# First rounds of attention in another order: second keys and queries loaded ahead of v, unit 2's scores ahead of v's pooling, weights converted later

## The chip, the core and the metric

The kernel runs on one NeuronCore of a Trainium2 chip. Five engines each work through their own list in order: TensorE (PE in the profile, PEld for its weight loads), VectorE (DVE), ScalarE (ACT), GpSimd (POOL), and SyncE (SP), whose queue issues the DMAs. Semaphores tie them together. The metric is device time in microseconds (us) of one execution; before the change the median of three runs is 660.65 us (657.95 to 663.04).

## What is computed

```python
def _attn_ref(q, k, v):                     # (2, 8, 576, 64)
    q_d, k_d, v_d = (t.reshape(B, H, Sd, 4, D).mean(axis=3) for t in (q, k, v))
    out_up = np.repeat(sm_attn(q_d, k_d, v_d), 4, axis=2)
    mask = np.abs(pos[:, None] - pos[None, :]) < 4
    scores = np.where(mask, scale * q @ k.T, -1e9)
    return out_up + softmax(scores) @ v
def reference(...):
    x = attn_out                            # 1152 tokens x 512
    h = x @ w_in                            # 512 -> 2048
    x = (h * clip(h + 3, 0, 6) / 6) @ w_out
    return sum(p[:, e] * (relu(x @ w1[e]) @ w2[e]) for e in range(4))
```

Two batches of eight heads. Each head has a local attention (each token sees the three before and after it) and a pooled one over means of four tokens; the sum goes through one wide MLP and then four weighted ones.

## The kernel before, in words

Products that need fp32 accuracy are made of a high and a low half of each operand (`three`: high-high, high-low, low-high). The long part of the run is the MLPs, one unbroken row of such matmuls. The change lies ahead of it, in the attention.

**Units and rounds.** A unit is two heads of one batch: eight units, 0 to 3 of batch 0, 4 to 7 of batch 1. Keys and queries are loaded for two units at a time (a pair, `load_k`, `load_q`; pair 0 in two pieces), v for a batch in three tiles (`load_v`, six to nine DMAs). A unit's work is cut into steps, and the loop over `t` (rounds 0 to 9) writes the steps of up to four units beside each other:

- `sums`: pooled keys and queries (sums of four), on POOL, or for the keys of the first units on DVE.
- `masks`, `scores` (L594, L607): local scores in PSUM, over a mask. `pooled_scores` (L670).
- `pooled_softmax` (L683 to L695), `less_max` (L624 to L631), `normalise`, `pooled_normalise`: maxima and sums on DVE, exponentials on ACT, the multiplications by the reciprocal on POOL.
- `turn` (L654), `pooled_turn` (L724): transposes on PE, copied to SBUF by ACT (`aT`, `aTd`).
- `values` (L744, L755): both attentions times v; then ACT copies the pooled part (`pd`), DVE adds (`xf`, L769), ACT rounds to the high half of x, and `low` (L785) makes the low half on DVE.
- `pool_v` (L463): sums of four rows of v, 18 matmuls for a batch, copied by ACT (L471). Its PSUM room is the single buffer called "last", which `values` and the idle products of round 1 use too; all else rotates through three buffers.

In these phases the order on PE, DVE, ACT and POOL is the order in which the program is written. SP's order is made by a scheduler. `idle_products(ps, n)` puts n matmuls of zeros (L551) into PE's list; nothing reads them.

**Conversion.** Each 1 MB tile of `w_in` arrives in a packed form and goes through a generator (`converting`) of four steps a tile: L237 on DVE with L213 on ACT; L247 on DVE; L259 and L268 on DVE with the high half on ACT (L221); the low half on DVE (L226). `convert(n)` runs the next n steps. Weight 0 is first needed by the matmuls of `pieces(1)` in round 8, weight 1 in round 9. The two first tiles are loaded in halves (`load_half`); these and the loads of the second batch are held: a one-element write of DVE (`hold`, L181) at the place where `load_next` calls them has to come before the DMA.

## Time and profile before

| | |
|---|---|
| median of three runs | 660.65 us |
| the profiled execution | 657.16 us, of which the trace spans 655.0 us |
| PE busy | 647.4 us (99%) |
| DVE, ACT, POOL busy | 415.9, 253.3, 95.3 us |
| granted TensorE clock, mean | 1.000 |

A busy PE here includes idle products, which do nothing for the result. The attention's rounds fill about the first 76 us.

### The profile page before, as it was taken

The page shows a single profiled execution, that of the slowest core. Times are in us where ns is not written, and L with a number is a line of the kernel's source. Part 1 is how long each engine was busy: PE and PEld are TensorE (multiplying, and loading weights), DVE is VectorE, ACT ScalarE, POOL GpSimd, SP SyncE. Part 2 cuts the span into 40 slices and gives each one's busy share as a digit, 9 for nine tenths or more (in the row PEclk, how much of TensorE's full clock was granted, in tenths as well). Part 3 has the DMA queues.
Part 4 walks back from the last instruction along what each step waited for, and adds up shares of the span by engine and source line. Part 5 has one row for each costly group of instructions (what it writes and reads, how often), then busy time and mean ns, then how long its engine had stood idle before and what let it go on. Part 6 is the DMA issues. An engine that isn't in the chain of part 4 may idle for free.

```text
span 655.0 us, 11972 instructions
## 1 busy us (share of the span) xinstructions
PE 647.4 (99%) x4929; PEld 582.6 (89%) x4943; DVE 415.9 (63%) x839; ACT 253.3 (39%) x591; POOL 95.3 (15%) x142
## 2 busy tenths in 40 slices
PE   8999999999999999999999999999999999999997
PEld 4657999999999999998998998998998988988985
DVE  6578899852794247585665665665765665755742
ACT  5567577442554246343233232241341331331410
POOL 4762000000000062101201201201201201201000
PEclk9999999999999999999999999999999999999999
DMA  8772333300510110300110110110210300200012
GB/s 278 226 236 91 130 124 134 129 1 1 193 66 1 65 64 1 131 2 0 65 65 1 65 65 1 65 65 1 87 43 0 129 2 15 115 1 2 2 48 97
DMA packets 12147, 45.89 MB, mean 70 GB/s; under 512 B 1334, under 2 KB 3382, under 8 KB 8252
## 3 DMA queue, kind: packets, MB, share of 16 engines
q1 hardware_dynamic: 12092, 45.12, 20.3%
q8 instruction: 39, 0.64, 0.4%
q14 instruction: 16, 0.13, 0.1%
HBM read 42.76 MB, written 2.36 MB: 69 GB/s over the span
## 4 chain that ended last, share of the span: by engine, by line
PE 96%; DMA 2%; SPq 1%; issue 0%; POOL 0%; DVE 0%; POOLq 0%
PE bank L936 27%; PE bank L1205 10%; PE bank L1206 10%; PE bank L1204 10%; PE bank L374 10%; PE bank L376 10%; PE bank L375 10%; PE pair L744 2%; PE pair L551 1%; DMA slot<-in_qT_dram 1%; PE pair L755 1%; DMA slot<-in_v_dram 1%; PE pair L607 1%; PE pair L724 1%; PE pair L670 1%; PE pair L654 1%
## 5 line engine op out<-in xcount | busy, mean ns | idle before, releaser
L936 PEld LDWEIGHTS bank<-xop,slot 128*128 128x128 f32 x1344 | 180.9, 188 | 1.3
L936 PE MATMUL bank<-xop,slot 128*128 128x288 f32 x1344 | 181.8, 295 | 0.0
L1205 PE MATMUL bank<-slot,h 128*128 128x512 f32 x288 | 113.9, 395 | 0.0
L1206 PE MATMUL bank<-slot,h 128*128 128x512 f32 x288 | 113.9, 395 | 0.0
L1204 PE MATMUL bank<-slot,h 128*128 128x512 f32 x288 | 113.8, 395 | 0.0
L1212 DVE SCALAR_TENSOR_TENSOR slot<-bank,pr,slot 128x512 f32<-128x512 f32 x63 | 47.3, 751 | 85.8 <-PE bank L1206 85.8
L442 POOL TENSOR_TENSOR st<-slot 128x256 f32<-128x256 f32 x16 | 13.9, 868 | 467.4 <-DMA slot<-in_w_dram 220.5
L1206 PEld LDWEIGHTS bank<-slot,h 128*128 128x128 f32 x288 | 54.1, 188 | 13.0
L1205 PEld LDWEIGHTS bank<-slot,h 128*128 128x128 f32 x288 | 54.1, 188 | 12.4
L1204 PEld LDWEIGHTS bank<-slot,h 128*128 128x128 f32 x288 | 54.1, 188 | 12.3
L376 PE MATMUL bank<-h,slot 128*128 128x384 f32 x192 | 64.7, 337 | 0.0
L375 PE MATMUL bank<-h,slot 128*128 128x384 f32 x192 | 64.7, 337 | 0.0
L374 PE MATMUL bank<-h,slot 128*128 128x384 f32 x192 | 64.7, 337 | 0.0
L374 PE MATMUL bank<-x,slot 128*128 128x384 f32 x188 | 63.1, 336 | 0.0
L376 PE MATMUL bank<-x,slot 128*128 128x384 f32 x188 | 62.9, 335 | 0.0
L375 PE MATMUL bank<-x,slot 128*128 128x384 f32 x188 | 62.9, 335 | 0.0
L442 DVE TENSOR_TENSOR u<-bank,u 128x288 f32<-128x288 f32 x96 | 43.6, 454 | 20.4 <-PE bank L936 20.0
L965 ACT ACTIVATE h<-c 128x288 fp32r<-128x288 f32 x64 | 27.9, 445 | 71.6 <-DVE c L442 71.5
L304 ACT ACTIVATE slot<-st 128x512 fp32r<-128x512 f32 x32 | 19.2, 624 | 64.6 <-POOL st L298 64.6
L825 DVE TENSOR_TENSOR h<-slot,h 128x384 fp32r<-128x384 f32 x48 | 27.5, 585 | 24.2 <-ACT h L824 24.1
L816 ACT ACTIVATE t<-bank,half__145 128x384 f32<-128x384 f32 x47 | 27.1, 581 | 40.1 <-PE bank L376 40.1
L817 DVE SCALAR_TENSOR_TENSOR slot<-t,bank 128x384 f32<-128x384 f32 x47 | 25.8, 552 | 24.5 <-ACT t L816 24.3
(115 smaller groups left out, 920.1 us busy)
## 6 DMA issues: line engine op xcount, KB each, us to landing
slot<-in_w_dram SPq DMA_DIRECT2D x16, 1024.0 KB, 4.8
slot<-in_w_out_dram SPq DMA_DIRECT2D x8, 1024.0 KB, 4.8
slot<-in_w_in_dram SPq DMA_DIRECT2D x6, 1024.0 KB, 5.3
slot<-in_v_dram SPq DMA_DIRECT2D x6, 512.0 KB, 4.8
out_dram<-slot SPq DMA_DIRECT2D x9, 256.0 KB, 2.0
slot<-in_w_in_dram SPq DMA_DIRECT2D x4, 512.0 KB, 5.9
slot<-in_kT_dram SPq DMA_DIRECT2D x3, 576.0 KB, 5.6
slot<-in_qT_dram SPq DMA_DIRECT2D x6, 288.0 KB, 6.0
```

The costliest lines, as they stand in the source:

```text
L374: nc.tensor.matmul(ps, wh, xh, start=first, stop=False)
L375: nc.tensor.matmul(ps, wh, xl, start=False, stop=False)
L376: nc.tensor.matmul(ps, wl, xh, start=False, stop=last)
L442: eng.tensor_tensor(out=out, in0=a, in1=b, op=ALU.add)
L816: nc.scalar.activation(out=t, in_=ps, func=AF.Relu, bias=half_, scale=1.0 / (6.0 * UP))
L825: nc.vector.tensor_tensor(out=g[:, 1, :], in0=u, in1=r32(g[:, 0, :]), op=ALU.subtract)
L936: nc.tensor.matmul(ps, a[:, i, k], b[:, j, k], start=start and k == 0 and n == 0, stop=stop and k == 1 and n == 2, skip_group_check=True,)
L965: nc.scalar.activation(out=self.h[:, 0, i, j], in_=of, func=AF.Relu)
L1204: nc.tensor.matmul(ps, hh, w[:, 0], start=(f == 0), stop=False)
L1205: nc.tensor.matmul(ps, hh, w[:, 1], start=False, stop=False)
L1206: nc.tensor.matmul(ps, hl, w[:, 0], start=False, stop=(f == NF - 1))
L1212: nc.vector.scalar_tensor_tensor(out=to, in0=ps, scalar=share, in1=to, op0=ALU.mult, op1=ALU.add)
```

## The change

In the first four rounds the steps stand in another order; in all rounds the loop is written out anew. `BY_DVE` is 4, and `sums` is split into `sums_k` (keys; on DVE for units 0 to 3) and `sums_q` (queries, on POOL).

```diff
     load_qk(0, 0, 1)
     load_qk(0, 1, 1)
+    load_qk(1)
     for p in range(NP):
         load_v(0, p)
-    load_qk(1)
...
-                if self.u < 2:
+                if self.u < BY_DVE:
                     nc.vector.tensor_reduce(out=to, in_=k4[:, r, : NI - r], op=ALU.add, axis=AX.X)
...
     later = [
-        lambda: load_half(0, 0),
-        lambda: load_half(0, 1),
         lambda: load_v(1, 0, (0,)),
         lambda: load_v(1, 0, (1,)),
         lambda: load_v(1, 1, (0,)),
-        last_v,
         lambda: load_k(NU // 2 - 1, held=True),
         lambda: load_q(NU // 2 - 1, held=True),
+        last_v,
+        lambda: load_half(0, 0),
+        lambda: load_half(0, 1),
         lambda: load_half(1, 0),
         lambda: load_half(1, 1),
     ]
...
+        elif t == 1:
+            n.pooled_scores(4)
+            n.masks(0)
+            n.scores()
+            n.pooled_softmax()
+            units[0].pooled_normalise()
+            load_qk(2)
+            units[2].sums_q()
+            n.less_max()
+            n.normalise()
+            n.pooled_normalise()
+            units[2].sums_k()
+            units[3].sums_k()
+            units[3].sums_q()
+            units[0].turn(0)
+            idle_products(banks(True), 8)
+            units[0].pooled_turn()
+            n.turn(4)
+        elif t == 2:
+            n.masks(0)
+            n.scores()
+            n.pooled_scores(0)
+            n.less_max()
+            n.pooled_softmax()
+            load_next()
+            n.normalise()
+            n.pooled_normalise()
+            load_next()
+            units[1].pooled_turn()
+        elif t == 3:
+            n.pooled_scores(0)
+            pool_v(0)
+            n.masks(0)
+            n.scores()
+            n.pooled_softmax()
+            units[4].sums()
+            n.less_max()
+            load_next()
+            n.normalise()
+            units[0].values()
+            units[2].turn(0)
+            units[2].pooled_turn()
+            n.pooled_normalise()
+            load_next()
+            units[5].sums()
+        elif t < NU:
+            n.pooled_scores(4)
+            n.masks(0)
+            n.scores()
+            n.pooled_softmax()
+            load_next()
+            n.less_max()
+            if t == NHP + 1:
+                pool_v(1)
+                convert(2)
+            units[0 if t == NHP else t - 3].low()
+            n.pooled_normalise()
+            n.normalise()
+            load_next()
+            if t < NU - 2:
+                units[t + 2].sums()
+            if t == NHP:
+                units[1].values()
+            units[t - 1].turn(4)
+            units[t - 2].values()
+            if t == NHP:
+                units[1].low()
+            units[t - 1].pooled_turn()
+            convert(1 if t > NHP else 0)
+            load_next()
...
```

Before, every round from 1 to 7 had the second form without its special cases, `pool_v(0, 8)` stood in round 1, `values` of unit t-2 in round t from 2 on, and `convert` ran 2 steps in round 3, one each in rounds 4 to 7, and 3 each in rounds 8 and 9; now it runs 3, 1, 1, 4 and 3 in rounds 5 to 9. Both make 12 steps. The idle products in PE's list were 71 and are 59: round 1 has 16 (before: 4, and 8 ahead of the pooling), rounds 2 and 3 have none (before: 8 each), rounds 4 to 7 have 8 each as before. At the end of round 4, PE has in both forms done the same work otherwise.

SP's queue, from the second load of pair 0's keys on; `in_kT_dram 128x2x576` is a pair's keys, `in_qT_dram 128x2x288` half a pair's queries. Before:

```order
L391 DMA slot<-in_kT_dram 128x576
L401 DMA slot<-in_qT_dram 128x288 x2
L410 DMA slot<-in_v_dram 48x512
L410 DMA slot<-in_v_dram 64x512
L410 DMA slot<-in_v_dram 128x512
L410 DMA slot<-in_v_dram 128x2x512 x3
L410 DMA slot<-in_v_dram 48x512
L410 DMA slot<-in_v_dram 32x512
L410 DMA slot<-in_v_dram 3x512
L391 DMA slot<-in_kT_dram 128x2x576
L401 DMA slot<-in_qT_dram 128x2x288 x4
```

Now:

```order
L393 DMA slot<-in_kT_dram 128x576
L403 DMA slot<-in_qT_dram 128x288 x2
L393 DMA slot<-in_kT_dram 128x2x576
L403 DMA slot<-in_qT_dram 128x2x288 x2
L412 DMA slot<-in_v_dram 48x512
L412 DMA slot<-in_v_dram 64x512
L412 DMA slot<-in_v_dram 128x512
L412 DMA slot<-in_v_dram 128x2x512 x3
L412 DMA slot<-in_v_dram 48x512
L412 DMA slot<-in_v_dram 32x512
L412 DMA slot<-in_v_dram 3x512
```

Pair 1's three loads (1152 KB) stand ahead of the nine loads of v's first batch (2182 KB) instead of behind them.

DVE's list in round 4, from unit 4's pooled denominators on; `den` to `rec` are of unit 4's softmax, `xf` is the sum that frees the PSUM room of `values`. Before:

```order
L706 TENSOR_SCALAR den_792<-smd_776 72x4
L710 RECIPROCAL recd_794<-den_792 72x4
L636 TENSOR_REDUCE sm_797<-ex1_125 128x10
L638 RECIPROCAL rec_799<-sm_797 128x10
L181 MEMSET slot_782 1x1
L769 TENSOR_TENSOR xf_871<-pair_828,pd_869 128x5x64
L769 TENSOR_TENSOR xf_871<-pair_828,pd_869 128x4x64
L247 SCALAR_TENSOR_TENSOR slot_712<-slot_445,slot_712 128x512 x2
```

Now:

```order
L718 TENSOR_SCALAR den_718<-smd_705 72x4
L722 RECIPROCAL recd_720<-den_718 72x4
L648 TENSOR_REDUCE sm_723<-ex1_125 128x10
L650 RECIPROCAL rec_725<-sm_723 128x10
L183 MEMSET slot_555 1x1
L438 MEMSET slot_730 6x512
L781 TENSOR_TENSOR xf_783<-pair_740,pd_781 128x5x64
L781 TENSOR_TENSOR xf_783<-pair_740,pd_781 128x4x64
L781 TENSOR_TENSOR xf_848<-pair_805,pd_846 128x5x64
L781 TENSOR_TENSOR xf_848<-pair_805,pd_846 128x4x64
```

There are two `xf` (of units 1 and 2) instead of one, and a hold and the zeroing of v's last rows (L436, now L438) stand between the reciprocal and the first of them.

DVE's list in rounds 7 and 8; L237 to L226 (now L239 to L228) are conversion. Before, weight 0's L226 stands a round earlier and is not in the piece, and `slot_1489` is weight 1:

```order
L769 TENSOR_TENSOR xf_1367<-pair_1324,pd_1365 128x5x64
L769 TENSOR_TENSOR xf_1367<-pair_1324,pd_1365 128x4x64
L237 TENSOR_SCALAR slot_1230<-slot_889 128x1024
L785 TENSOR_TENSOR x_78<-xf_1367,x_78 128x576
L817 SCALAR_TENSOR_TENSOR slot_1404<-t_1402,pair_1389 128x384
L769 TENSOR_TENSOR xf_1449<-pair_1406,pd_1447 128x5x64
L769 TENSOR_TENSOR xf_1449<-pair_1406,pd_1447 128x4x64
L247 SCALAR_TENSOR_TENSOR slot_1230<-slot_889,slot_1230 128x512 x2
L259 TENSOR_SCALAR slot_1230<-slot_1230 128x1024
L268 TENSOR_TENSOR slot_1230<-slot_1230 128x512 x2
L237 TENSOR_SCALAR slot_1580<-slot_1481 128x1024
L226 TENSOR_TENSOR slot_1489<-slot_1230,slot_1489 128x512 x2
```

Now, with `slot_1210` weight 0 and `slot_1476` weight 1:

```order
L781 TENSOR_TENSOR xf_1347<-pair_1304,pd_1345 128x4x64
L228 TENSOR_TENSOR slot_1210<-slot_953,slot_1210 128x512 x2
L797 TENSOR_TENSOR x_78<-xf_1347,x_78 128x576
L829 SCALAR_TENSOR_TENSOR slot_1390<-t_1388,pair_1375 128x384
L781 TENSOR_TENSOR xf_1435<-pair_1392,pd_1433 128x5x64
L781 TENSOR_TENSOR xf_1435<-pair_1392,pd_1433 128x4x64
L239 TENSOR_SCALAR slot_1367<-slot_968 128x1024
L249 SCALAR_TENSOR_TENSOR slot_1367<-slot_968,slot_1367 128x512 x2
L261 TENSOR_SCALAR slot_1367<-slot_1367 128x1024
L270 TENSOR_TENSOR slot_1367<-slot_1367 128x512 x2
L239 TENSOR_SCALAR slot_1567<-slot_1468 128x1024
L228 TENSOR_TENSOR slot_1476<-slot_1367,slot_1476 128x512 x2
```

Weight 0's low half is made behind round 7's `xf`, where weight 1's first step stood, and that step stands behind round 8's first `xf`.

## Rows read from the trace of the kernel before

**Rows 1.** The page, part 4: the chain that ended last, shares by engine.

```profile
PE 96%; DMA 2%; SPq 1%; issue 0%; POOL 0%; DVE 0%; POOLq 0%
```

**Rows 2.** Windows: us PE, PEld, DVE, ACT, POOL busy (x count), PEclk, DMA share, GB/s.

```profile
10.00:20.00 10.00, 8.76 (x140) 3.97 (x142) 3.89 (x12) 5.74 (x23) 4.47 (x10) 1.00 0.87 285
80.00:90.00 10.00, 10.00 (x60) 10.00 (x59) 9.94 (x19) 7.73 (x15) 0.00 (x0) 1.00 0.31 106
```

**Rows 3.** Timeline, rounds 1 to 4: start, us, engine, line, out<-in, count [idle <-releaser].

```profile
11.62 0.56 PE L654 MATMUL pair<-ident,ex 64*128 64x64 f32 x10 [0.75 <-POOL ex L640]
13.94 4.06 PE L463 MATMUL pair<-slot,fours 38*32 38x512 f32 x36
19.88 0.71 PE L670 MATMUL pair<-slot 64*72 64x144 f32 x8 [0.38 <-POOL slot L442]
20.52 0.34 PE L594 MATMUL pair<-mask,identb 128*128 128x190 bf16 x2
21.57 1.04 PE L551 MATMUL pair<-zeros 128*128 128x512 bf16 x3
23.05 1.35 PE L744 MATMUL pair<-aT,slot 38*64 38x32 f32 x72
25.12 0.70 PE L724 MATMUL pair<-ident,exd 72*80 72x72 f32 x8
25.66 1.03 PE L551 MATMUL pair<-zeros 128*128 128x512 bf16 x3
26.62 0.71 PE L670 MATMUL pair<-slot 64*72 64x144 f32 x8
40.46 0.71 PE L670 MATMUL pair<-slot 64*72 64x144 f32 x8
```

**Rows 4.** Timeline of POOL: the sums that wait for keys and queries.

```profile
7.32 1.17 POOL L442 TENSOR_TENSOR slot<-slot 128x288 f32<-128x288 f32 x2 [0.83 <-DMA slot<-in_qT_dram]
16.95 1.31 POOL L442 TENSOR_TENSOR slot<-slot 128x288 f32<-128x288 f32 x3 [3.78 <-DMA slot<-in_kT_dram]
18.65 1.17 POOL L442 TENSOR_TENSOR slot<-slot 128x288 f32<-128x288 f32 x2 [0.39 <-DMA slot<-in_qT_dram]
```

**Rows 5.** Timeline: pooling of v without a wait, and the copies after the first.

```profile
42.06 3.64 PE L463 MATMUL pair<-slot,fours 38*32 38x512 f32 x36
18.05 1.07 ACT L471 ACTIVATE slot<-pair 80x512 f32<-80x512 f32 x2 [3.81 <-PE pair L463]
```

**Rows 6.** Timeline of DVE, rounds 3 and 4: what stands around xf.

```profile
28.44 0.54 DVE L624 TENSOR_REDUCE mx<-pair 128x10 f32<-128x380 f32 x1
31.29 0.22 DVE L638 RECIPROCAL rec<-sm 128x10 f32<-128x10 f32 x1
32.72 0.82 DVE L769 TENSOR_TENSOR xf<-pair,pd 128x320 f32<-128x320 f32 x2 [0.76 <-ACT pd L763]
34.44 0.48 DVE L436 MEMSET slot<- 6x512 f32 x1 [0.17 <-issue]
```

**Rows 7.** Tile in_w_in_dram: from issue to landing of its loads.

```profile
DMA to landing us min/median/max: 4.5/5.7/8.3
```

**Rows 8.** Timeline, rounds 6 to 9: low halves of weights, and their readers.

```profile
57.46 1.28 DVE L226 TENSOR_TENSOR slot<-slot 128x512 fp32r<-128x512 f32 x2
63.47 0.82 DVE L769 TENSOR_TENSOR xf<-pair,pd 128x320 f32<-128x320 f32 x2 [0.73 <-ACT pd L763]
63.90 0.35 PE L376 MATMUL pair<-x,slot 128*128 128x384 f32 x1
65.75 1.24 PEld L744 LDWEIGHTS pair<-aT,slot 38*64 38x64 f32 x72 [0.25 <-ACT aTd L732]
72.79 1.29 DVE L226 TENSOR_TENSOR slot<-slot 128x512 fp32r<-128x512 f32 x2 [0.18 <-ACT slot L221]
73.65 0.34 PE L376 MATMUL bank<-x,slot 128*128 128x384 f32 x1
87.42 1.29 DVE L226 TENSOR_TENSOR slot<-slot 128x512 fp32r<-128x512 f32 x2
```

## The prediction

> **What bounds the kernel now.** I read the chain of waits first: 96% of the time to the end is PE's own work [rows 1]. The table of windows says where something else could still matter. In 10 to 20 us PE is busy 8.76 of 10 us and moves only 140 matmuls; in 80 to 90 us it is an unbroken row, and DVE is busy 9.94 of 10 us beside it [rows 2]. So only what shortens or breaks PE's row counts, and nearly all of the change lies ahead of 76 us. The timeline of rounds 1 to 4 shows what PE's row is made of. Between unit 0's transposes at 11.62 and round 5's pooled scores at 40.46 lie 28.84 us [rows 3]; both forms do the same useful work in this stretch, so I compare its length.

> One round, read off as differences of starts [rows 3]: pooled scores 0.64 (19.88 to 20.52), masks and scores 1.05 (to 21.57), four idle products and the transposes 1.48 (to 23.05), values 2.07 (to 25.12), pooled transposes 0.54 (to 25.66), four idle products 0.96 (to 26.62).

> **What goes.** Twelve idle products less, three groups of 0.96: 2.9 us. They are on the path, since PE goes through its list in order; what they covered has to be looked at below. The pooling of v took 4.06 us in round 1, where it waited for v, and takes 3.64 us in round 5 [rows 3, 5]: 0.4 us, if v has landed when PE comes to it. The 0.38 us that unit 2's pooled scores waited for POOL at 19.88 [rows 3]; POOL itself had waited 3.78 us for pair 1's keys [rows 4]. Together 3.7 us.

> The long wait of POOL thus hid nearly all behind PE's pooling. That is why loading pair 1 early is worth 0.4 us and not 4.

> **Whether the loads arrive.** Pair 0's last queries had landed at 7.32, and pair 1's keys at 16.95, behind 2182 KB of v and 576 KB of their own: 286 KB per us [rows 4]. Now pair 1 (1152 KB) lands at about 11.4 and v at about 19.0. PE comes to the pooling at 11.62 + 2.32 (to 13.94) + 0.54 + 1.48 + 1.05 + 0.64 + 0.54 + 0.64 = 18.8 [rows 3]. Pair 1 is in time by some 2 us. v is just in time: I count no wait, and there is no cover. Pair 1's key sums are four reductions more on DVE and two fewer groups of sums on POOL, both while PE does idle products and transposes: nothing on the path.

> **New waits up to round 5.** The pooling now stands behind unit 3's pooled scores, and unit 0's values need its copies (1.07 us, [rows 5]) out of the same PSUM buffer; masks and scores cover 1.05 of about 1.1: 0.1 us. Round 4's masks need the PSUM buffer of unit 2's transposes, whose copies stand on ACT behind unit 0's x. No row shows that wait; it lies between 0 and one pair of copies, 1.07 us [rows 5]. By my count of starts it is 0.3 us, nearer to 0.

> Round 4 does two values. The second needs the PSUM buffer that the first's xf frees, and this xf stands on DVE behind unit 4's whole softmax and a zeroing. From the end of scores PE needs 2.07 + 1.48 = 3.55 us to get there. DVE needs: scores end at 26.62 + 1.69 = 28.31 in the round shown, the reciprocal ends at 31.51, then 0.5 for the zeroing and 0.8 for xf [rows 3, 6]: about 4.6 us with a hold between. A wait of 1.1 us, with nothing to cover it; the four idle products that stand in it are already counted.

> Round 5 starts 3.7 - 0.1 - 0.3 - 1.1 = 2.2 us earlier, at 38.3.

> **Rounds 5 to 7.** PE's order is as before. Weight 0's halves are held until round 5 now, and DVE's L239 and ACT's copy of them stand in the row ahead of round 5's other work. The second half is issued about 1.8 us into round 5, at 40.1, and lands 4.5 to 8.3 us later, median 5.7 [rows 7]: at 44.6 to 48.4. What covers it is the second pooling, 3.64 us [rows 5]. The first victim would be round 6's masks, due at 38.3 + 6.74 + 3.6 + 0.64 = 49.3, behind 2.1 us of ACT's copies: landing by 47.2 costs nothing. With the median it is 45.8, so I count 0.

> **Rounds 8 and 9.** Weight 0's low half was made at 57.46, six us ahead of its reader at 63.90 [rows 8]. Now it stands behind the xf that starts at 63.47: 0.82 of xf and half of 1.28 put its first half at about 65.0. The reader waits 1.1 us. PE's 0.25 us wait at 65.75 for ACT goes with it [rows 8]. Weight 1's low half started at 72.79, its first half was there at about 73.45, and its reader came at 73.65 [rows 8]: 0.2 us of slack. Now one more conversion step, L239, stands ahead of it on DVE: one instruction, between 0.64 and 1.28, which are one and both of L226's two [rows 8]. I take 0.64, less 0.2 of slack: 0.4 late. After that the twelve steps have all been run as before. Weight 2 is ready at 88.7 (87.42 + 1.29), and PE needs it ten pieces of twelve matmuls after 73.2; at 60 matmuls per 10 us [rows 2, 8] that is 93: a busy DVE has some 4 us in hand, so being 1 us earlier costs nothing.

> **Sum.** -2.2 + 1.1 - 0.25 + 0.4 = -0.95 us. Against the profiled execution's own 657.16 that is 656.2; this execution lies 3.5 us under the median of the three runs, 660.65, so the median should be **659.7 us**, 0.14% less.

> [...]

> **Rivals.**
> - *The new waits are not there* (20%): PE's row closes up in round 4 and in rounds 8 and 9, because DVE is less loaded than I count. For it: conversion has left rounds 3 and 4. Against: xf and the low halves stand where they stand in DVE's list. Then 3.7 + 0.25 = 4.0 us are gained: 656.7.
> - *Weight 0 comes late* (15%, slower): it decides from a landing later than 47.2. At the slowest landing seen, 48.4, ACT's copies make round 6's masks 1.2 us late, and the pooled copies behind them make the next reuse of a PSUM buffer late by about as much again: 2.4 us, so -0.95 + 2.4, some 1.5 us slower: 662.1. For it: both queues would stand still behind one DMA. Against: nothing else is in the DMA queue by then.
> - *The clock falls in rounds 2 and 3* (5%, slower): without idle products PE waits there. The two rounds hold about 10 us of matmuls (two scores 2.1, pooled scores 1.3, pooling 3.64, values 2.07, transposes 1.6); at half clock they cost up to 10 more, at none of it 0. Halfway, 5 us: 664.7.
> - *The change doesn't do what it says* (10%): v, pushed back by 1152 KB, is not there when PE comes to it at 18.8. The two loads together move 3334 KB from 7.32 on; at a rate 10% under 286 KB per us v lands 1.3 us later, and the gain is gone: 661.0.
> - The forecast keeps 50%, with a range of its own of 658.7 to 660.7.

> **The numbers.** The range reaches from the first rival to the fourth and the second, and the three runs of before lie up to 2.7 us from their median: 656.3 to 663.2. It leaves out the clock's case and the tails of the runs. One per cent is 6.6 us, about what a measurement of this kernel can tell from no change. The gain can't reach that, since only 4 us are removed; 4% for what I don't see. Slower by as much takes the clock's case at its full price or two rivals together: 6%. Within 1%: 90%.

> **What would show it.** In the changed trace: unit 2's scores at about 16, with no wait of POOL for pair 1; the pooling at about 19 in under 3.8 us; a wait of about 1 us ahead of round 4's second values, released by DVE's xf; round 5's pooled scores near 38.3; the third matmul of round 8's first piece a good 1 us behind its first, released by DVE's L228; the first L376-to-L378 group of weight 1 a few tenths late; clock 1.00 in every window. Round 5's start outside 37 to 40, a wait of PE for a DMA, or a clock under 1.00 would make the prediction wrong at that step; a wait in rounds 5 to 7 behind ACT or DVE would make the second rival right.

## The result and the profile after

The changed kernel takes 664.07 us (median of 14 executions, 661.14 to 668.34), the kernel before 657.92 in 14 executions beside it: ratio 1.0097, 95% interval [1.0077, 1.0116]. Forecast were 659.7 us and a gain of 0.95 us; it is a loss of 6.15. Of the 14 executions not one has a mean granted clock of 1.00 (0.982 to 0.995), and by and large the lower the clock, the longer the time. (Executions more than 1.5% above the fastest of the same kernel are left out of every ratio here.) The profiled execution has 663.88 us, a span of 661.8 against 655.0 before.

The chain of waits, by engine; it was 96% PE and 0% DVE [rows 1]:

```profile
PE 92%; DVE 5%; issue 1%; DMA 1%; ACT 0%; POOL 0%; DVEq 0%; ACTq 0%; POOLq 0%
```

Windows of the changed kernel, columns as in [rows 2]; the column behind the busy times is the granted clock:

```profile
15.00:20.00 5.00, 4.88 (x122) 3.23 (x125) 3.71 (x11) 2.30 (x8) 2.92 (x4) 1.00 1.07 304
20.00:25.00 5.00, 4.08 (x108) 1.52 (x97) 3.61 (x8) 2.51 (x11) 3.40 (x6) 1.00 0.83 231
25.00:30.00 5.00, 3.61 (x107) 2.55 (x94) 1.88 (x5) 2.18 (x11) 1.63 (x3) 0.75 0.50 171
30.00:35.00 5.00, 5.00 (x64) 3.12 (x65) 1.48 (x6) 2.18 (x6) 3.23 (x8) 0.57 0.20 56
65.00:70.00 5.00, 3.40 (x36) 2.64 (x35) 4.77 (x10) 4.11 (x13) 1.93 (x2) 0.84 0.35 144
70.00:75.00 5.00, 5.00 (x103) 4.22 (x102) 0.88 (x2) 0.98 (x3) 0.00 (x0) 0.81 0.01 3
```

In windows of one microsecond the clock is 0.50 from 28 to 34 us and from 69 to 71. A mean of 0.75 over 5 us is 2.5 us at 0.50, 0.57 is 4.3: some 6.8 us at half clock (0.50) around 30 us, and 3.5 around 70. PE stood, that is started nothing, just ahead of each fall (4.08, 3.61 and 3.40 of 5 us busy). Where, the timeline of PE shows (columns as in [rows 3], whose rows these answer):

```profile
16.34 0.34 PE L606 MATMUL pair<-mask,identb 128*128 128x190 bf16 x2
...
18.78 0.71 PE L682 MATMUL pair<-slot 64*72 64x144 f32 x8
19.42 2.78 PE L465 MATMUL pair<-slot,fours 38*32 38x512 f32 x28
23.12 1.06 PE L465 MATMUL pair<-slot,fours 38*32 38x512 f32 x8 [0.92 <-issue]
24.11 0.34 PE L606 MATMUL pair<-mask,identb 128*128 128x190 bf16 x2
24.38 0.84 PE L619 MATMUL pair<-slot 64*32 64x38 f32 x72
25.36 0.90 PE L756 MATMUL pair<-aT,slot 38*64 38x32 f32 x46
27.50 1.07 PE L756 MATMUL pair<-aT,slot 38*64 38x32 f32 x26 [1.25 <-issue]
...
33.51 1.08 PE L682 MATMUL pair<-slot 64*72 64x144 f32 x8
...
40.20 1.35 PE L756 MATMUL pair<-aT,slot 38*64 38x32 f32 x72 [1.01 <-DVE xf L781]
...
43.77 0.71 PE L682 MATMUL pair<-slot 64*72 64x144 f32 x8
...
66.56 0.42 PE L376 MATMUL pair<-x,slot 128*128 128x384 f32 x1
...
68.76 0.69 PE L378 MATMUL pair<-x,slot 128*128 128x384 f32 x1 [1.60 <-DVE slot L228]
...
75.19 0.42 PE L376 MATMUL bank<-x,slot 128*128 128x384 f32 x1
...
80.35 0.44 PE L378 MATMUL bank<-x,slot 128*128 128x384 f32 x1 [0.18 <-DVE slot L228]
```

Two waits are the predicted ones (1.01 for unit 1's xf, 1.60 for weight 0's low half). Two were in no term of the sum: PE stands 0.92 us inside the pooling of v and 1.25 us inside unit 0's values, and the profile shows nothing that it waited for ("issue"). Count what lies between. An f32 product leaves two MATMUL records and two weight loads here, so four instructions (values: 36 products per unit, 72 MATMUL records; scores: 36 products, 72 and 72). From one stand to the next: 8 + 8 of the pooling, 2 + 2 masks, 72 + 72 scores, 46 + 46 values: **256 instructions**. I call such a stretch a block and its two ends block ends. Counted back by another 256, the block ahead of the first stand begins about with unit 2's masks, at 16.34 (252 instructions from there by the records). And 46 records are 23 products, an odd number: the second stand lies between the two heads of one window, which read the same tiles, so it cannot be a wait for data.

The DMA view of two short stretches shows a packet of another kind there, 16 KB on the queue named "instruction" (38 of them carry 0.62 MB in the whole run, and PE's 9862 records of matmuls and loads make 260 for each). Before, 18.4 to 18.6 us:

```profile
DMA packets 14, 0.03 MB, mean 140 GB/s; under 512 B 3, under 2 KB 13, under 8 KB 13
q8 instruction: 1, 0.02, 33.1%
```

After, 20.2 to 20.4 us; the next one lies between 25.0 and 25.2:

```profile
DMA packets 45, 0.07 MB, mean 363 GB/s; under 512 B 6, under 2 KB 31, under 8 KB 44
q8 instruction: 1, 0.02, 37.4%
```

Before, the engines were nearly empty when it ran (share 0.25 from 18 to 19 us); after, they are full from 10 us to 20 (share 1.04 and 1.07), because pair 2's keys (576 KB) are now issued at 14.0 us and not at 19.9, and v's second batch behind them from 17.2 on and not from 20.9. PE was in the block that begins at 16.34 when this packet ran, 4.0 us behind its start.

### The profile page after: what moved, and what is told of

It reads as the page before. It is cut to its first block, busy times and chain, and to the rows that moved or that the text cites. A ratio compares the mean times of both kernels' runs of the same rounds, so it can differ in the third digit from the quotient of the medians.

```text
span 661.8 us, 11968 instructions
## 1 busy us (share of the span) xinstructions
PE 650.2 (98%) x4931; PEld 584.9 (88%) x4931; DVE 418.8 (63%) x843; ACT 253.6 (38%) x591; POOL 93.3 (14%) x136
## 4 chain that ended last, share of the span: by engine, by line
PE 92%; DVE 5%; issue 1%; DMA 1%; ACT 0%; POOL 0%; DVEq 0%; ACTq 0%; POOLq 0%
PE bank L948 27%; PE bank L1261 10%; PE bank L1262 10%; PE bank L1260 10%; PE bank L378 10%; PE bank L376 10%; PE bank L377 10%; PE pair L553 1%; DMA slot<-in_w_in_dram 1%; PE pair L756 1%; PE pair L465 1%; DVE slot L249 1%; DVE xf L781 1%; DVE mxd L695 1%; PE pair L682 0%
## 5 line engine op out<-in xcount | busy, mean ns | idle before, releaser
L378 PE MATMUL bank<-h,slot 128*128 128x384 f32 x192 | 64.7, 337 | 0.0
L376 PE MATMUL bank<-h,slot 128*128 128x384 f32 x192 | 64.7, 337 | 0.0
L378 PE MATMUL bank<-x,slot 128*128 128x384 f32 x188 | 63.0, 335 | 0.2 <-DVE slot L228 0.2
L376 PE MATMUL bank<-x,slot 128*128 128x384 f32 x188 | 63.1, 336 | 0.0
L837 DVE TENSOR_TENSOR h<-slot,h 128x384 fp32r<-128x384 f32 x48 | 27.5, 584 | 24.3 <-ACT h L836 24.2
L828 ACT ACTIVATE t<-bank,half__145 128x384 f32<-128x384 f32 x47 | 27.1, 581 | 38.4 <-PE bank L378 38.3
```

The source lines that it names most:

```text
L376: nc.tensor.matmul(ps, wh, xh, start=first, stop=False)
L378: nc.tensor.matmul(ps, wl, xh, start=False, stop=last)
L828: nc.scalar.activation(out=t, in_=ps, func=AF.Relu, bias=half_, scale=1.0 / (6.0 * UP))
L837: nc.vector.tensor_tensor(out=g[:, 1, :], in0=u, in1=r32(g[:, 0, :]), op=ALU.subtract)
```

## Experiments

Each kernel is timed against the kernel before on the same chip. Lines named in a diff are those of the changed kernel unless it says otherwise.

**12 idle products back in round 3.**

```diff
-            pool_v(0)
-            n.masks(0)
+            pool_v(0, 4)
+            n.masks(8)
```

> The changed kernel with 12 idle products put back in round 3: 4 ahead of the pooling of v, 8 ahead of unit 3's masks. Theory (PE stood 0.92 us in the pooling and 1.25 us in unit 0's values with nothing to wait for but its own instructions, the granted clock then fell to half from 27.5 to 34.3 us, and this is what round 5's start lost): the 8 products, 1.7 us, lie where PE stood 1.25 us and 0.26 us, the clock stays at 1.00 from 20 to 60 us, round 5's pooled scores start at about 41.5 instead of 43.8, and the time is 661.5 to 662.5 us (ratio to the changed kernel 0.996 to 0.998). Rival (the low clock cost nothing, since the softmax chain set the pace there): the products come on top, pooled scores of round 5 at 44 to 45.5, time 664 to 666 us.

Measured: 662.76 us, ratio 1.0073 [1.0044, 1.0101]. Timeline of PE:

```profile
23.12 1.91 PE L465 MATMUL pair<-slot,fours 38*32 38x512 f32 x12 [0.15 <-issue]
...
27.73 1.35 PE L756 MATMUL pair<-aT,slot 38*64 38x32 f32 x72
...
31.81 0.71 PE L682 MATMUL pair<-slot 64*72 64x144 f32 x8
...
38.53 1.45 PE L756 MATMUL pair<-aT,slot 38*64 38x32 f32 x72 [1.33 <-DVE xf L781]
...
44.00 1.24 PE L682 MATMUL pair<-slot 64*72 64x144 f32 x8
```

The first stand is met with 12 records left and not 8: two products, 8 instructions earlier, as the 4 added products (a load and a matmul each) make it. The second is gone, and round 4 starts at 31.81, not 33.51: up to there the products paid for themselves. But the clock, 1.00 from 20 to 40 us, now falls at 40, behind the wait for xf (0.50 from 40 to 45 us; 0.71 becomes 1.24 in the last row), and round 5 starts as late as ever. The theory was right on the stands and missed that the clock falls behind the next wait instead.

**Weight 0's low half earlier in round 7.**

```diff
             n.less_max()
+            if t == NU - 1:
+                convert(1)
...
-            convert(1 if t > NHP else 0)
+            convert(1 if NHP < t < NU - 1 else 0)
```

> The changed kernel with one conversion step moved inside round 7: the subtraction that makes weight 0's low half stands right behind the unit's maximum subtraction instead of at the round's end behind unit 5's x rows. Theory (the wait of 1.60 us in round 8's first weight product for that subtraction, and the half clock from 68.4 to 71.9 us behind it, are a second loss of 1.6 + about 1.4 us): the wait is under 0.4 us, the clock does not fall there, time about 661 us, ratio to the changed kernel 0.9945 to 0.997. Rival (DVE is the bound of round 7, so the wait moves to the normalisation of unit 7 and its turn in round 8): the gain is at most 1.3 us, 662.7 to 664 us.

Measured: 660.53 us, ratio 1.0052 [1.0027, 1.0078]. Timeline of PE:

```profile
22.38 1.06 PE L465 MATMUL pair<-slot,fours 38*32 38x512 f32 x8 [0.20 <-issue]
...
27.04 1.07 PE L756 MATMUL pair<-aT,slot 38*64 38x32 f32 x26 [1.52 <-issue]
...
65.91 0.42 PE L376 MATMUL pair<-x,slot 128*128 128x384 f32 x1
...
66.34 0.34 PE L378 MATMUL pair<-x,slot 128*128 128x384 f32 x1
...
71.29 0.42 PE L376 MATMUL bank<-x,slot 128*128 128x384 f32 x1
```

The wait is gone, and so is the fall behind it (clock 1.00 from 65 to 75 us): between the two weight pieces PE needs 5.38 us and not 8.63. These 3.2 us are what comes back in the time too, some 3 us by the two ratios, as expected. The two stands lie at the same two products as in the changed kernel.

**Both.** The two diffs above together.

> The changed kernel with both: 12 idle products in round 3 and weight 0's subtraction earlier in round 7. Theory (two separate losses that add): granted clock 1.00 from 10 to 80 us and 658 to 660 us, level with the kernel before (657.9). Rival (one of the two gives back nothing once the other is gone, since both ends wait for the same loads): 661 to 662.5 us.

Measured: 661.33 us, ratio 1.0038 [1.0018, 1.0057], not to be told from the second alone: the rival's range. The profile shows why: the clock falls at 40.0 us (0.50 from 40 to 45) behind the 1.33 us wait for xf, as with the idle products alone.

**Block ends shifted by 28 instructions.** In round 0, two of eleven idle products are cut into 16 of an eighth of the columns:

```diff
-            idle_products(self.sc, idle)
+            idle_products(self.sc, idle - 2 if idle == IDLE else idle)
+            if idle == IDLE:
+                for n in range(16):
+                    at = n % 8 * 64
+                    nc.tensor.matmul(self.sc[:, n // 8, at : at + 64], zeros[:, :P],
+                                     zeros[:, at : at + 64], start=True, stop=True)
```

> The changed kernel with two of the eleven idle products of round 0 cut into 16 of 64 columns: the same columns, but 14 products, 28 PE instructions, more ahead of everything else. Theory (PE's two stands lie at the end of a block of its instruction stream, 256 instructions apart: 4 products of the pooling, the masks, 36 scores and 23 products of values at 4 instructions each, 2 to 4 for masks, come to 256): both stands move 28 instructions, 7 products, earlier: the pooling stops after 7 of its 18 products (14 records in place of 28) and unit 0's values after 16 of 36 (32 records in place of 46). Rival (a load of v that lands late): the stands stay where they are, ahead of the same products.

Measured: 660.28 us (one execution). Timeline of PE, with one row of its weight loads (lines are 10 higher here):

```profile
19.41 4.51 PE L465 MATMUL pair<-slot,fours 38*32 38x512 f32 x36
21.16 0.27 PEld L465 LDWEIGHTS pair<-slot,fours 38*32 38x32 f32 x10 [0.75 <-issue]
...
25.09 1.35 PE L766 MATMUL pair<-aT,slot 38*64 38x32 f32 x72
...
35.87 1.53 PE L766 MATMUL pair<-aT,slot 38*64 38x32 f32 x72 [1.32 <-DVE xf L791]
```

The second stand is gone. The first moved to where the theory had it, and shrank: PE's row doesn't mark it, but the pooling takes 4.51 us and not 3.64 [rows 5], and its weight loads stop for 0.75 us, for nothing shown, behind 15 of 36 (expected were 14, before 28). No load and no dependency was changed, so the rival (late v) falls. The instruction packet ran between 18.6 and 18.8 us, 1.6 earlier, and PE is in the block 1.6 earlier: counted back, it begins at 14.7, among the idle products of round 1, and the packet runs 3.9 us behind that, as it ran 4.0 before. My reading: idle products take 0.24 us for two instructions (0.96 for four of them; values 1.29 for 144 instructions), so a block that has some lasts longer and the next has more time to come. That the second stand went for this reason is argued. The clock falls again behind the wait of 1.32 us for xf: round 5's pooled scores, at 41.22, take 1.24 us and not 0.71.

**Idle products in the wait for xf.** Block ends shifted, weight 0 earlier, and in round 4:

```diff
-            units[t - 1].turn(4)
+            units[t - 1].turn(10 if t == NHP else 4)
```

> The changed kernel with two idle products of round 0 cut into 16 (28 instructions more ahead), weight 0's subtraction earlier in round 7, and 10 idle products in place of 4 in unit 3's turn in round 4, ahead of unit 2's values, which waited 1.0 to 1.3 us for the x rows of unit 1. Theory (what was lost is PE standing long enough to lose the clock, at three places: the block ends of its instructions, the wait for the x rows in round 4, the wait for weight 0; the order itself is worth its gain): clock 1.00 from 10 to 650 us, round 5's pooled scores at 38.3 to 39.0, time 655 to 656.5 us, ratio to the kernel before 0.995 to 0.998. Rival (the wait for the x rows sets round 5 with or without the clock): pooled scores at 40.5 or later, 657.5 to 659 us.

Measured: 656.08 us, ratio 0.9982 [0.9958, 1.0007]; 8 of 11 executions at a clock of 0.999 or more. A window and the timeline of PE:

```profile
20.00:30.00 10.00, 9.87 (x291) 6.24 (x283) 6.69 (x19) 6.52 (x24) 6.75 (x12) 1.00 0.62 184
```

```profile
18.42 0.71 PE L692 MATMUL pair<-slot 64*72 64x144 f32 x8
...
28.24 0.71 PE L692 MATMUL pair<-slot 64*72 64x144 f32 x8
...
38.65 0.71 PE L692 MATMUL pair<-slot 64*72 64x144 f32 x8
```

Round 5 starts at 38.65, where the prediction had it (38.3), 5.1 us ahead of the changed kernel. Up to there the order is worth 1.8 us (before: 40.46) once PE neither stands nor loses its clock, the six idle products more included. The whole time isn't told apart from the kernel before.

**Pooled turn in that wait.** As before, with 7 idle products and the pooled turn moved ahead:

```diff
-            units[t - 1].turn(4)
+            units[t - 1].turn(7 if t == NHP else 4)
+            if t == NHP:
+                units[t - 1].pooled_turn()
             units[t - 2].values()
...
-            units[t - 1].pooled_turn()
+            if t > NHP:
+                units[t - 1].pooled_turn()
```

> As the kernel with 10 idle products in unit 3's turn, but with 7 there and unit 3's pooled turn (0.70 us of PE work) moved ahead of unit 2's values, so that work stands in the wait for the x rows. Theory: the same clock, 1.00 throughout, and up to 0.7 us less: 654.5 to 656 us. Rival (ScalarE's two copies of the pooled turn now lie ahead of unit 2's and delay the x rows of unit 2, on which round 5's values wait): no gain over the other, or up to 0.7 us more.

Measured: 658.22 us, ratio 0.9991 [0.9974, 1.0008]; 5 of 12 executions at 0.999 or more. No gain, more falls; the profiled execution stands 1.28 us at a block end in round 1. It doesn't separate theory and rival.

**The kernel before without the 16 idle products of rounds 2 and 3.**

```diff
-                n.pooled_scores(4)
+                n.pooled_scores(0 if t in (2, 3) else 4)
...
-            units[t - 1].turn(0 if t in (1, NU) else 4)
+            units[t - 1].turn(0 if t in (1, 2, 3, NU) else 4)
```

> The kernel before with nothing but the 16 idle products of rounds 2 and 3 taken out, 4 each ahead of units 2's and 3's pooled scores and of units 1's and 2's turns: a part of the change alone. The prediction's price (12 products 2.9 us, 0.24 us each) gives 16 x 0.24 = 3.9 us at most, 654 us. Theory (dense PE work there runs to the end of an instruction block before the next block has come, and other waits appear, and the clock falls): one stand of 0.5 to 1.5 us with nothing shown as its cause between 18 and 35 us, or a fall of the granted clock there, and 657 to 660 us, no gain. Rival (the idle products cost what they take): 654 to 655.5 us at clock 1.00.

Measured: 658.98 us, ratio 1.0020 [0.9994, 1.0047]. Timeline of PE:

```profile
15.53 2.79 PE L463 MATMUL pair<-slot,fours 38*16 38x512 f32 x28 [1.02 <-DMA slot<-in_v_dram]
20.04 0.71 PE L670 MATMUL pair<-slot 64*72 64x144 f32 x8 [1.09 <-POOL slot L442]
32.24 0.33 PE L724 MATMUL pair<-ident,exd 72*64 72x72 f32 x1 [0.85 <-issue]
```

As the theory said: a stand of 0.85 and falls of the clock (0.66 and 0.70 in the windows from 25 to 35 us) eat a saving priced at 3.9 us. The first fall, at 25.2 us, stands behind waits for v and for POOL of 1.02 and 1.09 us and ahead of the stand, so it isn't the stand's. Taking idle products out is worth nothing in either order by itself.

**Pair 2's loads behind unit 3's q sums.** Its keys and half of its queries (864 KB) are issued at 18.1 and 18.6 us then; the other half waits for nothing there and goes at 11.7. All else as changed.

```diff
-            load_qk(2)
             units[2].sums_q()
...
             units[3].sums_q()
+            load_qk(2)
```

> The changed kernel with the loads of pair 2 issued behind unit 3's q sums in round 1 (18.0 us) in place of ahead of unit 2's (13.5 us); every other transfer keeps its place in the queue. Theory (PE's first stand is a 16 KB piece of its instructions, whose packet ran at 20.37 us behind data that kept the DMA engines full from 10 to 22 us): the packet runs at 18.0 to 18.8 us, as in the kernel before (18.49), the stand of 0.92 us in the pooling vanishes, the second stand, where the packet runs 1.3 to 2 us after the block is entered, stays or is up to 1 us shorter; time 661.5 to 663.5 us. Rival (the packet's time has nothing to do with the data): packet at 20 us or later, both stands as they are, 663.5 to 665 us.

Measured: 661.33 us, ratio 1.0059 [1.0024, 1.0093]. The instruction packet between 17.2 and 17.4 us, and PE:

```profile
DMA packets 13, 0.03 MB, mean 149 GB/s; under 512 B 2, under 2 KB 10, under 8 KB 12
q8 instruction: 1, 0.02, 33.2%
```

```profile
16.35 0.34 PE L606 MATMUL pair<-mask,identb 128*128 128x190 bf16 x2
...
19.44 3.64 PE L465 MATMUL pair<-slot,fours 38*32 38x512 f32 x36
...
24.27 1.35 PE L756 MATMUL pair<-aT,slot 38*64 38x32 f32 x72 [0.15 <-ACT slot L473]
...
35.07 1.35 PE L756 MATMUL pair<-aT,slot 38*64 38x32 f32 x72 [1.33 <-DVE xf L781]
39.19 1.24 PE L682 MATMUL pair<-slot 64*72 64x144 f32 x8
```

PE is at the block's start as before (16.35 and 16.34). With the DMA engines nearly empty (share 0.24 from 17 to 18 us) the packet runs 1.0 us behind it in place of 4.0, and both stands are gone: the data ahead of it had delayed it, and with it, by my reading, PE's instructions. At the next packet a full share did not make it late: it ran at 22.38, 0.75 us behind its block's start, at a share of 1.03 to 1.10. (One stand of 0.81 us shows at a later block end, at 62 us.) The second stand going as well was not expected. The clock is lost at 38 us, behind xf (the pooled scores at 39.19 take 1.24 us and not 0.71), and again behind weight 0 (a wait of 0.88 us, then weight products of 0.52 us and not 0.34).

**The same, with weight 0 earlier, xf's wait left.**

> The changed kernel with pair 2's loads behind unit 3's q sums and weight 0's subtraction earlier in round 7; the wait for unit 1's x rows ahead of unit 2's values left as it is. Theory (that wait of 1.0 to 1.3 us alone is enough to lose the clock, though nothing stands before it): no stand from 15 to 30 us, the clock falls to half between 36 and 39 us, round 5's pooled scores at 39 to 41.5, time 657.5 to 659.5 us. Rival (the fall at 38.0 us in the kernel with the loads moved needs the stands before): clock 1.00 throughout, 656 to 657 us.

Measured: 660.35 us, ratio 1.0034 [1.0012, 1.0057]; no execution at 0.999. In this profile a stand of 0.46 us is back at the block end in unit 0's values, and the clock falls there (0.54 from 25 to 30 us) and behind the 1.00 us wait for xf, to 0.50 in the whole window from 40 to 45 us. So neither prediction of the two held cleanly: here it fell behind both. It need not: behind the wait of 1.01 us for xf in the changed kernel it stayed at 1.00 (40 to 45 us).

**All three causes taken away:** pair 2's loads later, weight 0 earlier, 10 idle products ahead of unit 2's values.

> As the kernel before it in this list, with 10 idle products in place of 4 in unit 3's turn, ahead of unit 2's values: all three causes taken away, without the cut idle products of round 0. Theory: clock 1.00 from 10 to 650 us, pooled scores of round 5 at 38.0 to 38.8, time 654.5 to 656.5 us, the ratio to the kernel before 0.995 to 0.998. Rival (the pieces of PE's instructions still come late in some executions, without the cut products): stands of 0.5 us or more between 15 and 30 us, 657 to 659 us.

Measured: 657.99 us, ratio 0.9978 [0.9955, 1.0000], the rival's range. At a clock of 0.999 or more it takes 653.99 to 655.54 us (3 executions of 11), where the kernel before takes 656.2 to 658.1; the others lose the clock. What PE shows ahead of the fall in the profiled one:

```profile
25.61 0.66 PE L756 MATMUL pair<-aT,slot 38*64 38x32 f32 x26 [0.29 <-issue]
```

The same block end, with 26 of 72 records to go, a stand of only 0.29, and the clock falls at 27.7 us (0.77 and 0.89 in the windows from 25 to 35 us).

**The same with the shift of 28 instructions.**

> As the kernel with all three causes taken away, and with two idle products of round 0 cut into 16, which shifts the block ends by 28 instructions. Theory (once the loads leave room, the shift is worth nothing): within 0.7 us of the kernel without it. Rival (both are needed): 0.7 to 2 us less than without it.

Measured: 657.31 us, ratio 0.9989 [0.9966, 1.0011], 3 of 12 executions at 1.00: within 0.7 us of the kernel without it. PE's row marks no stand, yet the clock falls at 27.4 us. But the row of unit 0's values takes 1.65 us and not 1.35, and its weight loads show where:

```profile
24.95 0.78 PEld L766 LDWEIGHTS pair<-aT,slot 38*64 38x64 f32 x40 [0.20 <-issue]
```

40 of 72 are to go, so it is the shifted block end (32 = 46 - 14), and from record 32 to 33 PE starts nothing for 0.31 us. The shift moved this stand too.

**The same (without the shift) with the pooled turn ahead of unit 2's values.**

> As the kernel with all three causes taken away, but with 7 idle products in unit 3's turn and its pooled turn ahead of unit 2's values. Theory: 0 to 0.7 us less than with 10 idle products (654 to 656 us). Rival (the copies of the pooled turn delay unit 2's x rows): the same or up to 0.7 us more.

Measured: 658.48 us, ratio 0.9997 [0.9976, 1.0018], 2 of 11 executions at 1.00: the rival's side, no gain.

**4 idle products ahead of unit 3's masks**, on the kernel with all three causes taken away:

```diff
             pool_v(0)
-            n.masks(0)
+            n.masks(4)
```

> The kernel with all three causes taken away (pair 2's loads later, weight 0's subtraction earlier, 10 idle products ahead of unit 2's values) and with 4 idle products ahead of unit 3's masks in round 3. Theory (what still takes the clock in most executions, at 25 to 31 us, is the dense run of small products from unit 2's masks to unit 0's values, at whose end PE reaches a block end 0.3 to 1.0 us too early): the 4 products, 0.8 us, fill that stand, the clock is 1.00 from 10 to 650 us in most executions, median 654.5 to 656 us, 1.5 to 3 us under the kernel before. Rival (the stand is not what takes it): clock below 0.999 in most executions as without them, 657.5 to 659 us.

Measured: 656.80 us, ratio 0.9987 [0.9960, 1.0014], 6 of 12 executions at 1.00 in place of 3 of 11. It points the theory's way, too weakly to call it shown.

**The same 4 products on the kernel with shifted block ends**, pair 2's loads as changed:

> The kernel with the cut idle products of round 0 (28 instructions more ahead), weight 0's subtraction earlier and 10 idle products ahead of unit 2's values, pair 2's loads where the change put them, and with 4 idle products ahead of unit 3's masks. Theory: most executions at clock 1.00, median 655 to 656.5 us. Rival (late pieces of the instruction stream in some executions, since the loads leave no room): stands and 656.5 to 658.5 us.

Measured: 657.15 us against 658.25, ratio **0.9971 [0.9954, 0.9989]**, 9 of 12 executions at 0.999 or more: faster than both kernels, if by 0.3%. It is the lowest ratio of fifteen kernels and was not measured again. Most executions keep the clock, as the theory said; the time lies in the rival's range, and the profiled execution waits 0.65 us for v.

**The load order alone undone:** v ahead of pair 1 again.

```diff
-    load_qk(1)
     for p in range(NP):
         load_v(0, p)
+    load_qk(1)
```

> The changed kernel with the first v loaded ahead of pair 1 again, as before the change: the load order alone undone. Theory (the load order is worth what POOL and PE waited for pair 1, and the stands come from the dense products of rounds 2 and 3, whichever comes first): GpSimd waits 2 us or more for pair 1's keys, unit 2's q sums end at 18 us or later in place of 14.8, PE waits 2 to 3 us for unit 2's pooled scores and masks, the clock falls at 17 to 30 us, 665 to 668 us. Rival (the stands come from pair 1 ahead of v, which makes the transfers run together with PE's instructions): no stands in the pooling and unit 0's values, 658 to 662 us.

Measured: 672.91 us (four executions, 665.5 to 679.5), ratio 1.0175 [1.0126, 1.0225]. POOL and PE:

```profile
19.42 1.17 POOL L444 TENSOR_TENSOR slot<-slot 128x288 f32<-128x288 f32 x2 [6.55 <-DMA slot<-in_qT_dram]
```

```profile
21.43 0.90 PE L666 MATMUL pair<-ident,ex 64*128 64x64 f32 x10 [6.44 <-POOL ex L652]
```

Slower than both theories said, but for the profiled execution, the fastest: unit 1's normalisation stands behind unit 2's sums on POOL, and in PE's wait of 6.44 us the clock falls as well (0.88 from 15 to 20 us, 0.50 from 20 to 25). No stand shows in the pooling (at 26.5 us) and unit 0's values, which is the rival's sign; but both lie 6 to 7 us later here, so it doesn't decide what makes the stands. Pair 1 must come first once the pooling has left round 1.

## Why the prediction was wrong

The sum was made by starts of PE's row. In the prediction's own steps, with the two starts of before that no row above gives:

```profile
63.47 0.42 PE L374 MATMUL pair<-x,slot 128*128 128x384 f32 x1
...
68.84 0.42 PE L374 MATMUL bank<-x,slot 128*128 128x384 f32 x1
```

| Step | predicted | in the trace |
|---|---|---|
| start of round 5 (40.46 before, 43.77 after) | -2.2 | +3.3 |
| from there to weight 0's first piece (63.47, 66.56) | 0 | -0.2 |
| round 8, to the next piece (68.84, 75.19) | +0.85 | +3.3 |
| weight 1's low half and the rest | +0.4 | +0.4 (0.34 of it at the low half) |
| sum | -0.95 | +6.8, the spans' difference |

- **"Twelve idle products less: 2.9 us"** is the step that failed. They were counted as pure length. With twelve of them back in round 3 the first stand was 0.15 us and not 0.92, the second was gone, and the clock was 1.00 from 20 to 40 us, where the changed kernel has 0.75 and 0.57 from 25 to 35: by my reading they had also given PE's instructions time to come. Between the pooled scores of units 3 and 4 the changed kernel needs 33.51 - 18.78 = 14.73 us; the kernel without stands at full clock needs 28.24 - 18.42 = 9.82. Of these 4.9 us the stands are 2.2 and the half clock the other 2.7, the remainder.
- **"The clock falls in rounds 2 and 3"** had 5% and 664.7 us. No row of before shows a clock under 1.00, so the half clock in its price was my assumption; the changed kernel shows 0.50 from 28 to 34 us. The effect is right, in rounds 3 and 4; that the total came out near its 664.7 is half chance, since 2.4 of the loss are round 8's. It was priced as a risk by itself; it came with the stands and, in five of eight traces that have it, with the wait of 1.0 to 1.3 us for xf. Its chance was too low: the trace's clock of 1.00 [rows 2] was read off a stretch that still had its idle products. With 10 idle products in the wait for xf the clock stayed at 1.00 behind it (30 to 50 us), where it had fallen at 40.0 us with both diffs and at 38.0 with pair 2's loads later.
- **Loads.** v was there (no wait of PE on it in the changed kernel, 0.65 us in the last but one experiment, so it is as close as said); POOL's wait for pair 1 is gone. What was overlooked is that pair 2's keys are pulled from 19.9 to 14.0 us with it, and what else uses the DMA engines.
- **New waits.** The 1.1 us for xf is there (1.01); behind it the clock fell in other versions (0.50 from 40 to 45 us with the idle products of round 3). Round 5 starts at 38.65 when the falls and stands are out, 1.8 us earlier than before: the order's own gain of 2.2 us was nearly right.
- **Rounds 5 to 7.** Weight 0's late landing was hidden, as said.
- **Round 8.** The mechanism was right, the size off: 1.60 us and not 1.1, and the half clock behind it about as much again. The 0.25 us that were to go with it weren't there: 65.75 is a row of weight loads, and PE's own row goes from the last weight product to the values in 0.27 us before and in 0.29 after. Weight 1's 0.4 was right: its third product starts 0.52 us behind the second, where it had been 0.18.
- **The base.** 659.7 was worked out from the median of three executions, 660.65. In the comparison the kernel before takes 657.92, so the miss is 7.1 us and not 4.4.

Open: why, with all waits filled, the clock still falls in a quarter to three quarters of the executions. The kernel before loses it too, in 6 of 24 on one chip and 11 of 23 on another. The traces say where: of the fifteen changed forms six have a gap of 0.29 us or more at the block end in unit 0's values, and these six lose the clock between 24 and 28 us; no other form does. That is a match of single executions and no experiment; for the executions without a trace the cause stays open, and that 4 idle products help is not settled.

## What to carry to other kernels

Products that compute nothing may carry something: before taking them out, look at what PE does around them, at its clock and at how fast it would then run through its instructions. Small f32 products use them up fastest here (four each, 256 in 3.1 us), and with pair 2's keys ahead of it the packet of the next ones ran 4.0 us behind its block's start and not 1.0. The wait of 1.0 to 1.3 us for xf, among small products, cost twice in five of the eight traces that have it: itself (1.33 us with the idle products of round 3) and the half clock behind it (0.50 from 40 to 45 us). Filling it brought the clock back in round 4 (1.00 from 30 to 50 us), and moving the late step did in round 8 (1.00 from 65 to 75 us).
